# Retention attention in 64-token sub-chunks on quadrants of the PE array, four units moved to the second token chunk, and every queue's order planned and pinned

## The chip, the cores and the metric

The kernel runs on one core of a Trainium2 chip. The metric is the device time of one execution in microseconds (us). The kernel before takes 617.95 us, the median of 3 runs (617.76 to 618.27).

## What is computed

The reference is a retention layer (attention with an exponentially fading state) for 2 batches, 8 heads, 768 tokens and a head size of 64, followed by two feed-forward layers over all 1536 tokens. Weights and inputs are given in float64 and split on the chip into words that the engines can use.

```python
for t in range(S):                       # retention, per batch and head
    state = gamma * state + outer(k[t], v[t])
    y[t] = scale * q[t] @ state
x = y.transpose(...).reshape(1536, 512)
h = x @ moe_w_in                         # 512 -> 2048
g = softplus(h); x = g @ moe_w_out       # 2048 -> 512
h = x @ moe2_w_in
g = h * clip(h + 3, 0, 6) / 6; out = g @ moe2_w_out
```

## The kernel before

The token dimension is cut in three chunks of 512 (c = 0, 1, 2) for the feed-forward layers, and in 12 units of 128 tokens for the attention; units 0 to 3 make chunk 0, units 4 to 7 chunk 1, units 8 to 11 chunk 2. Units 0 to 5 belong to the first batch, 6 to 11 to the second.

**Feed-forward.** A layer m runs, for each chunk, 16 steps f of 128 hidden columns. `gemm1` makes one bank of hidden values from 12 matmuls of 128 x 512 (four k-slices, three products of high and low parts), then ScalarE (ACT) and VectorE (DVE) make g and its parts `hi` and `lo`. `gemm2` of the step two before (`LAG`) adds 12 more matmuls into four accumulating banks. A group of 12 matmuls is called a block below; there are 2 x 3 x 16 x 2 = 192 blocks, 2304 matmuls in all.

**Weights.** Each of the 64 weight tiles comes as 512 KB of float64 words (`fetch` into `raw`, three buffers) and goes through `convert`: ACT scales the upper word, DVE clamps it, shifts it, merges the sign and the upper bits of the lower word (four DVE instructions, two of them with one operand and two with two), ACT writes the high part. The low part is a subtraction on GpSimd (POOL) for the first eight tiles; for the others ACT writes the negative and a DMA queued on POOL adds `w` onto it. The 32 tiles of layer 0 are all needed in the time of chunk 0.

**Attention.** For a unit, PE transposes k and q (4 matmuls of 128 x 128 each), `scores` multiplies them per head on 64 of the array's 128 rows, `carry` multiplies q with the state `bd`, `intra` multiplies the masked scores `pt` with v on 64 of the array's columns, and `state` makes the unit's own k-v product. DVE masks the scores, scales the result by `tq_sb` and adds to the state; POOL scales v by `tk_sb` (units 2 to 11), fades the state and makes `x_lo`.

**Order.** Units 0 to 3 run before the first block, in program order (`InOrder` pins each instruction while `nc.on` is true). After that the scheduler of the tile framework chooses each engine's order by the priority of the program, with units 4 to 11 written into the first eight steps of the feed-forward. Its pools give out buffers as they come free.

The trace names one line (L31, the wrapper of `InOrder`) for nearly every instruction; the tiles' names tell them apart. An fp32 matmul of the attention stands in the trace as two records, so 8 matmuls of `scores` are 16 records.

Of the kernel before, what the change touches and what calls it, by code (L numbers as in the profile page):

```python
# [16 lines left out]
P = 128  # L17

# [3 lines left out]
class InOrder:  # L22


    class Engine:
        def __init__(self, owner, engine):
            self.owner, self.engine = owner, engine

        def __getattr__(self, op):
            def call(*args, **kwargs):  # L30
                ins = getattr(self.engine, op)(*args, **kwargs)  # L31
                return self.owner.tc.keep_in_program_order(ins) if self.owner.on else ins
            return call

    def __init__(self, tc):
        self.tc, self.on = tc, True
        for e in ("tensor", "vector", "scalar", "gpsimd", "sync"):
            setattr(self, e, self.Engine(self, getattr(tc.nc, e)))
# [3 lines left out]
def kernel(ctx, tc, q, k, v, w1_in, w1_out, w2_in, w2_out, tq, tk, tc_, tg, out):  # L42
    nc = InOrder(tc)
# [9 lines left out]
    chunks1 = [(0, 0, 512), (1, 0, 512), (2, 0, 512)]  # L53
    chunks2 = [(0, 0, 512), (1, 0, 512), (2, 0, 512)]
    LAG = 2
    EARLY = 4
# [3 lines left out]
    xpool = ctx.enter_context(tc.tile_pool(name="xpool", bufs=1))  # L60
    x_hi = [xpool.tile([P, KD, CH], F32R, name=f"x_hi{c}") for c in range(NT // CH)]
    x_lo = [xpool.tile([P, KD, CH], F32R, name=f"x_lo{c}") for c in range(NT // CH)]

    win_p = ctx.enter_context(tc.tile_pool(name="win", bufs=NF))
    wout_p = ctx.enter_context(tc.tile_pool(name="wout", bufs=NF))
    psum = ctx.enter_context(tc.tile_pool(name="psum", bufs=1, space=PSUM))
    raw_p = ctx.enter_context(tc.tile_pool(name="raw", bufs=3))
    cv_p = ctx.enter_context(tc.tile_pool(name="cv", bufs=2))

    w_in_t, w_out_t, raws = {}, {}, {}  # L70
    words = {0: (w1_in.bitcast(U32), w1_out.bitcast(U32)), 1: (w2_in.bitcast(U32), w2_out.bitcast(U32))}

    def fetch(m, o, f):
        raw = raw_p.tile([P, CH, 2], U32, tag="raw", name="raw")
        src = words[m][o]
        if o:
            nc.sync.dma_start(out=raw.rearrange("p n t -> p (n t)"), in_=src[f * P:(f + 1) * P, :])
        else:
            nc.sync.dma_start(out=raw.rearrange("p (k n) t -> p k (n t)", k=KD),
                              in_=src[:, 2 * f * P:2 * (f + 1) * P].rearrange("(k p) f -> p k f", p=P))  # L80
        raws[m, o, f] = raw

    def convert(m, o, f):

        raw = raws.pop((m, o, f))
        low, y = raw[:, :, 0], raw[:, :, 1]

        w = cv_p.tile([P, CH], U32, tag="w", name="w")
        nc.scalar.activation(y.bitcast(F32), y.bitcast(F32), AF.Copy, scale=2.0 ** -112)
        nc.vector.tensor_scalar(y.bitcast(F32), y.bitcast(F32), -TOP, TOP, ALU.max, ALU.min)  # L90
        nc.vector.tensor_scalar(w, y, 3, None, ALU.logical_shift_left)
        nc.vector.scalar_tensor_tensor(w, y, 0x80000000, w, ALU.bitwise_and, ALU.bitwise_or)
        nc.vector.scalar_tensor_tensor(w, low, 29, w, ALU.logical_shift_right, ALU.bitwise_or)
        t = (wout_p if o else win_p).tile([P, 2, CH], F32R, tag="w", name="w_parts")
        if done[1] < 2 * EARLY:
            nc.scalar.activation(t[:, 0], w.bitcast(F32), AF.Copy)
            nc.gpsimd.tensor_tensor(t[:, 1], w.bitcast(F32), t[:, 0].bitcast(F32), ALU.subtract)
        else:
            nc.scalar.activation(t[:, 1], w.bitcast(F32), AF.Copy, scale=-1.0)
            nc.gpsimd.dma_start(out=t[:, 1].bitcast(F32), in_=w.bitcast(F32), accum_op=ALU.add)  # L100
            nc.scalar.activation(t[:, 0], w.bitcast(F32), AF.Copy)
        if o:
            w_out_t[m, f] = t
        else:
            w_in_t[m, f] = t.rearrange("p a (k n) -> p a k n", k=KD)

    NU = B * NCH
# [4 lines left out]
    done = [0, 0]  # L112

    def fetch_weights(n):
        while done[0] < min(len(order), n):
            fetch(*order[done[0]])
            done[0] += 1

    def feed(n):

        n = min(n, len(order))
        while done[1] < n:
            fetch_weights(done[1] + (1 if nc.on else 2))
            convert(*order[done[1]])
            done[1] += 1

    banks = psum.tile([P, 8, CH], F32, name="banks")
    free = list(range(8))

    def bank(hold=False):  # L130

        i = free.pop(0)
        if not hold:
            free.append(i)
            return banks[:, i, :]
        return i, banks[:, i, :]

    def release(i):
        free.append(i)

    def first(f):
        return EARLY + 2 * (f + 1) - max(0, f + 1 + EARLY - NF)

# [11 lines left out]
    while s < n_steps:  # L155
        step(s)
        s += 1


def attention(ctx, tc, nc, q, k, v, tq, tk, tcc, tg, x_hi, x_lo, CH, bank, feed, fetch_weights):  # L160
# [86 lines left out]
    def state(u):  # L247
        b, i = units[u]
        if i == NCH - 1:
            return  # L250
# [211 lines left out]
```

## Time and profile before

| | |
|---|---|
| time, median of 3 runs | 617.95 us |
| span of the profiled execution | 613.8 us |
| PE (matmul) busy | 598.1 us |
| DVE busy | 351.8 us |
| ACT busy | 275.9 us |
| POOL busy | 103.4 us |
| first feed-forward matmul | 34.24 us |
| last attention matmul ends | about 120 us |
| last matmul ends | about 610.1 us |

The page lists no time of the profiled execution beside its span; the span runs from the first to the last instruction, and the median of the runs is 4.15 us above it. Busy shares are averages over very different stages: up to 34 us there is attention alone, up to about 125 us attention mixed with the first feed-forward steps and the weights' conversion, then feed-forward alone. A PE that is shown busy can still be slowed by its clock or by matmuls that use half of the array.

### The profile page before, as it was taken

Reading aid. Unit: us, or ns where it says so; the run is one execution under the profiler, and the core shown is the slowest. Engines: PE = TensorE matmul, PEld = TensorE weight load, DVE = VectorE, ACT = ScalarE, POOL = GpSimd, SP = SyncE. Lnnn points to the kernel's source line nnn. Section 1 sums busy time; section 2 is a strip of 40 time slices with the busy share of each in tenths; the row PEclk is TensorE's granted clock in tenths of the full one; section 3 lists DMA queues with packets and bytes.
Section 4 is the critical chain, followed back from the end, with each engine's and each line's share of the span. In section 5 each row is a group of like instructions: output and inputs, shape, how many; then the busy total and the mean of one; then the engine's idle time right before and its main releaser. Section 6 shows DMA issues by size and latency. Waiting matters only on the chain.

```text
span 613.8 us, 7743 instructions
## 1 busy us (share of the span) xinstructions
PE 598.1 (97%) x2963; PEld 491.2 (80%) x2963; DVE 351.8 (57%) x583; ACT 275.9 (45%) x473; POOL 103.4 (17%) x110
## 2 busy tenths in 40 slices
PE   7988999999999999999999999999999999999997
PEld 6865778788788888888887878888888888888886
DVE  4589999999773334376667798832322222322223
ACT  3355475678563333465556687722222222222220
POOL 1745664432100000011111122200000000000000
PEclk9998999999999999999999999999999999999999
DMA  9998888799600000045566689600100000100001
GB/s 193 236 229 211 219 197 208 192 217 227 159 32 0 1 0 1 9 111 119 140 180 154 162 208 262 125 7 1 68 1 0 1 1 0 70 1 1 0 1 69
DMA packets 69510, 61.60 MB, mean 100 GB/s; under 512 B 40032, under 2 KB 56672, under 8 KB 69472
## 3 DMA queue, kind: packets, MB, share of 16 engines
q1 hardware_dynamic: 61408, 46.42, 26.6%
q0 software_dynamic: 8064, 14.68, 14.6%
q8 instruction: 23, 0.38, 0.3%
q14 instruction: 15, 0.12, 0.1%
HBM read 43.26 MB, written 3.15 MB: 76 GB/s over the span
## 4 chain that ended last, share of the span: by engine, by line
PE 66%; DVE 13%; issue 7%; DMA 6%; ACT 3%; POOL 2%; SPq 1%; DVEq 0%; POOLq 0%; ACTq 0%
PE banks L31 66%; DVE w L31 6%; DMA raw<-in_moe_w_in_dram 3%; DVE raw L31 2%; POOL w_parts L31 2%; DMA w_parts<-w 2%; DVE g L31 1%; SPq L31 1%; DVE pt L31 1%; DMA q<-in_q_dram 1%; DVE lo L31 1%; ACT e L31 1%; DVE e L31 1%; ACT raw L31 1%; ACT w_parts L31 1%
## 5 line engine op out<-in xcount | busy, mean ns | idle before, releaser
L31 PE MATMUL banks<-x_hi,w_parts 128*128 128x512 f32 x768 | 253.9, 391 | 2.4 <-POOL w_parts L31 1.2
L31 PEld LDWEIGHTS banks<-x_hi,w_parts 128*128 128x128 f32 x768 | 143.8, 188 | 34.4 <-POOL w_parts L31 2.1
L31 PE MATMUL banks<-x_lo,w_parts 128*128 128x512 f32 x384 | 149.6, 390 | 0.0
L31 PE MATMUL banks<-hi,w_parts 128*128 128x512 f32 x384 | 129.4, 397 | 0.9 <-POOL w_parts L31 0.8
L31 PE MATMUL banks<-w_parts,hi 128*128 128x512 f32 (+1 forms) x386 | 118.4, 388 | 0.7 <-DVE g L31 0.7
L31 DVE SCALAR_TENSOR_TENSOR g<-e,banks 128x512 f32<-128x512 f32 x48 | 33.0, 687 | 123.3 <-ACT e L31 123.3
L31 DVE SCALAR_TENSOR_TENSOR w<-raw,w 128x512 uint32<-128x512 uint32 x128 | 94.3, 738 | 1.6
L31 DVE TENSOR_TENSOR lo<-g,hi 128x512 fp32r<-128x512 f32 x96 | 66.3, 690 | 48.9 <-ACT hi L31 48.6
L31 POOL DMA_DIRECT2D w_parts<-w x56 | 49.3, 880 | 251.9 <-DVE e L31 98.7
L31 ACT ACTIVATE hi<-g 128x512 fp32r<-128x512 f32 x96 | 60.5, 630 | 65.0 <-DVE g L31 61.6
L31 ACT ACTIVATE e<-banks,three 128x512 f32<-128x512 f32 x48 | 32.9, 686 | 125.7 <-PE banks L31 125.7
L31 ACT ACTIVATE w_parts<-w 128x512 fp32r<-128x512 f32 x120 | 70.4, 625 | 39.2 <-DVE w L31 39.0
L31 PEld LDWEIGHTS banks<-hi,w_parts 128*128 128x128 f32 x384 | 72.8, 190 | 17.6 <-POOL w_parts L31 1.5
L31 PEld LDWEIGHTS banks<-w_parts,hi 128*128 128x128 f32 x386 | 72.3, 188 | 16.0 <-DVE g L31 1.1
L31 PEld LDWEIGHTS banks<-x_lo,w_parts 128*128 128x128 f32 x384 | 72.1, 188 | 14.9
L31 PE MATMUL banks<-lo,w_parts 128*128 128x512 f32 x192 | 75.6, 394 | 0.4 <-DVE lo L31 0.4
L31 PE MATMUL banks<-w_parts,lo 128*128 128x512 f32 (+1 forms) x193 | 74.9, 388 | 0.0
L31 DVE SCALAR_TENSOR_TENSOR e<-g,banks 128x512 f32<-128x512 f32 x48 | 32.7, 682 | 27.5 <-ACT g L31 27.5
L31 DVE TENSOR_TENSOR g<-g,e 128x512 f32<-128x512 f32 x48 | 34.4, 717 | 23.9 <-ACT e L31 23.5
L31 ACT ACTIVATE raw<-raw 128x512 f32<-128x512 f32 x64 | 42.2, 669 | 12.7 <-DMA raw<-in_moe_w_in_dram 12.7
L31 ACT ACTIVATE g<-banks 128x512 f32<-128x512 f32 x48 | 28.2, 587 | 36.5 <-PE banks L31 36.5
L31 PEld LDWEIGHTS banks<-lo,w_parts 128*128 128x128 f32 x192 | 36.5, 190 | 8.9 <-DVE lo L31 1.5
(45 smaller groups left out, 401.1 us busy)
## 6 DMA issues: line engine op xcount, KB each, us to landing
raw<-in_moe_w_in_dram SPq DMA_DIRECT2D x32, 512.0 KB, 4.2
raw<-in_moe_w_out_dram SPq DMA_DIRECT2D x32, 512.0 KB, 4.6
w_parts<-w POOLq DMA_DIRECT2D x56, 256.0 KB, 4.9
q<-in_q_dram SPq DMA_DIRECT2D x12, 256.0 KB, 5.3
v<-in_v_dram SPq DMA_DIRECT2D x12, 256.0 KB, 4.9
k<-in_k_dram SPq DMA_DIRECT2D x11, 256.0 KB, 5.3
out_dram<-ob SPq DMA_DIRECT2D x11, 256.0 KB, 2.0
k<-in_k_dram SPq DMA_DIRECT2D x2, 128.0 KB, 2.8
```

Of the source, the lines that this page charges most:

```text
L31: ins = getattr(self.engine, op)(*args, **kwargs)
```

## The change

The same outputs are computed by another arrangement:

- A class `Plan` takes the place of `InOrder`. Every piece of work is a task with an engine, a cost, the tasks it comes after, a due time, and the buffers it takes and gives. `Plan.run` walks through the tasks engine by engine, chooses the next by due time among those that could start, and emits it; every instruction's order is pinned. Buffers are fixed tiles (`room`), numbered by the plan.
- Attention: each unit of 128 tokens is worked in two halves of 64 tokens. `scores`, `product` (before: `state`), `carry` and `inner` (before: `intra`) are each 16 matmuls of 64 x 64 x 64, placed on quadrants of the array: two row halves times two column halves. In `scores`, `product` and `inner` four consecutive matmuls use four quadrants; in `carry` they use the two quadrants on the diagonal, for one half of the tokens and then the other. The state lives in compact [128, 4, 64] tiles and is updated twice per unit (`middle`, `total`, `faded`).
- Units 4 to 7 are spread over chunk 0 of layer 0, four gaps between blocks per unit; units 8 to 11 are spread over chunk 1.
- POOL does no arithmetic: v's scaling, the state's fading and `x_lo` are on DVE; the low part of 15 of the 32 layer-0 tiles is a DVE subtraction, and the other 17 and all of layer 1 go by the accumulating DMA. POOL still issues those DMAs.
- Weights: for three tiles of four, ACT makes the lower word's bits (`bits`) and DVE merges with two two-operand instructions and one clamp; the fourth keeps the four DVE instructions of before. The first three weights' loads stand ahead of the loads of v and k for unit 3. Layer-1 weights are fetched one or two per step from chunk 2 of layer 0 on.
- Softplus takes one DVE instruction with one operand and one with two ahead of `lo`, where it took two with two.

```diff
-class InOrder:
...
+class Plan:
...
-    def decayed(u):
-        vs = wk.tile([P, H, D], F32, tag="vs" + "0" * (u < START), name="vs", bufs=2)
-        (nc.vector if u < 2 else nc.gpsimd).tensor_tensor(
-            vs, nat["v", u], tk_sb.rearrange("p (h o) -> p h o", o=1).to_broadcast([P, H, D]), ALU.mult)
...
-        for j in range(NP):
-            for g in range(2):
-                r = slice(D * g, D * (g + 1))
-                nc.tensor.matmul(sc[g][:, j, :], kT[r, j, :], qT[r, j, :])
...
-        nc.gpsimd.tensor_tensor(lo, on, hi.bitcast(F32), ALU.subtract)
...
+    def BY_DVE(n):
+        return n < 6 or n < 2 * NF and n % 3 == 1
+
+    def BITS(n):
+        return n % 4 != 1
...
+    spread(range(START, FIRST), 0, 1.0)
+    spread(range(FIRST, NU), 2 * NF, 1.0)
...
+        t1 = nc.add("ACT", 0.57, scale, [t0], use - tail - 3.5)
+        t3 = nc.add("DVE", TS, clamp, [t1], use - tail - 2.5)
+        if BITS(number):
+            t2 = nc.add("ACT", 0.65, bits, [t0], use - tail - 3.0, take=cv)
+            t4 = nc.add("DVE", TT, sign, [t3, t2], use - tail - 2.0)
+            t5 = nc.add("DVE", TT, shift, [t4], use - tail - 1.3, give=[raw_k])
...
+        def scores():
+            for p in range(NP):
+                for j in range(2):
+                    for g in range(2):
+                        nc.tensor.matmul(sub(sc, g)[part[j], p, :], tile_of("kT")[part[g], p, part[j]], tile_of("qT")[part[g], p, part[j]])
...
+        def product():
+            for h in range(H):
+                g, p = h % 2, h // 2
+                for j in subs:
+                    nc.tensor.matmul(sub(ds, j)[part[g], p, :], tile_of("k")[part[j], h, :], tile_of("vs")[part[j], h, :])
...
+        def carry():
+            for j in range(int(first), 2):
+                w = at_slot(mid[1] if j else ("end", u - 1))
+                for p in range(NP):
+                    for g in range(2):
+                        nc.tensor.matmul(bank(("oc", u))[part[g], p, part[j]], w[part[g], p, :], tile_of("qT")[part[g], p, part[j]])
...
+        def inner():
+            for h in range(H):
+                g, p = h % 2, h // 2
+                for j in range(2):
+                    nc.tensor.matmul(sub(oi, j)[part[g], p, :], tile_of("vs")[part[j], h, :], tile_of("pt").rearrange(
+                        "p n (g t) -> p g n t", g=2)[part[j], g, p, :])
```

The order that the plan makes is shown at three places. The first is PE's queue in the attention of the first four units, before any feed-forward matmul. Before, one unit stands like this: `qT,kT` is scores, `ident,k` and `ident,q` are transposes, `qT,bd` is carry, `pt,vs` is intra and `vs,k` is state.

```order
L31 MATMUL banks<-qT,kT 128x128 x8
L31 MATMUL banks<-ident,k 128x128 x4
L31 MATMUL banks<-ident,q 128x128 x4
L31 MATMUL banks<-qT,bd_112 128x128 x4
L31 MATMUL banks<-pt,vs 64x128 x8
L31 MATMUL banks<-vs,k 128x128 x4
```

Now the same place, for unit 2 (its scores are the first row) and the start of unit 3; `st` is the state.

```order
L41 MATMUL banks<-qT_0_130,kT_0_129 64x64 x16
L41 MATMUL banks<-vs_0_132,k_2_125 64x64 x16
L41 MATMUL banks<-ident,q_0_120 128x128 x4
L41 MATMUL banks<-qT_0_130,st_136 64x64 x8
L41 MATMUL banks<-qT_0_130,st_137 64x64 x8
L41 MATMUL banks<-pt_0_134,vs_0_132 64x64 x16
L41 MATMUL banks<-ident,k_0_123 128x128 x4
L41 MATMUL banks<-vs_1_133,k_0_123 64x64 x16
L41 MATMUL banks<-qT_1_131,kT_0_129 64x64 x16
```

A unit's 24 matmuls of half or full array width became 64 of a quarter, the k-v product moved ahead of the carry, and unit 3's transpose of k stands behind all of unit 2.

The second place is PE's queue in the middle of chunk 0, where unit 5's scores stand. Before:

```order
L31 MATMUL banks<-qT,kT 128x128 x4
L31 MATMUL banks<-hi,w_parts 128x512
L31 MATMUL banks<-lo,w_parts 128x512
L31 MATMUL banks<-qT,kT 128x128 x4
L31 MATMUL banks<-qT,bd_113 128x128 x4
L31 MATMUL banks<-pt,vs 64x128
L31 MATMUL banks<-vs,k 128x128 x4
L31 MATMUL banks<-pt,vs 64x128 x7
```

Now, between the last matmul of one block and the first of the next but one:

```order
L41 MATMUL banks<-x_hi_66,w_84 128x512
L41 MATMUL banks<-qT_1_131,kT_0_129 64x64 x16
L41 MATMUL banks<-qT_1_131,st_138 64x64 x8
L41 MATMUL banks<-qT_1_131,st_136 64x64 x8
L41 MATMUL banks<-pt_1_135,vs_1_133 64x64 x16
L41 MATMUL banks<-hi_109,w_87 128x512
```

The scheduler had split the scores into two runs, each on one row half, with feed-forward matmuls between them; now each part of a unit stands whole, between blocks.

The third place is DVE's queue in chunk 0, where weights are converted beside the softplus. Before (`raw` and `w` are a weight's words, `e` and `g` the softplus):

```order
L31 SCALAR_TENSOR_TENSOR e<-g,banks 128x512
L31 TENSOR_SCALAR w<-raw 128x512
L31 TENSOR_SCALAR raw<-raw 128x512
L31 SCALAR_TENSOR_TENSOR w<-raw,w 128x512
L31 TENSOR_TENSOR g<-g,e 128x512
L31 TENSOR_SCALAR w<-raw 128x512
L31 SCALAR_TENSOR_TENSOR w<-raw,w 128x512 x2
L31 TENSOR_TENSOR lo<-g,hi 128x512
```

Now (`cv` is the word being merged, `w` the finished tile whose low part DVE subtracts):

```order
L41 TENSOR_SCALAR raw_0_72<-raw_0_72 128x512
L41 SCALAR_TENSOR_TENSOR cv_1_76<-raw_0_72,cv_1_76 128x512 x2
L41 TENSOR_TENSOR w_93<-cv_0_75,w_93 128x512
L41 TENSOR_SCALAR e_104<-g_106 128x512
L41 TENSOR_TENSOR vs_1_133<-v_1_127,small 128x512
L41 TENSOR_SCALAR raw_1_73<-raw_1_73 128x512
L41 TENSOR_SCALAR cv_3_78<-raw_1_73 128x512
L41 SCALAR_TENSOR_TENSOR g_106<-g_106,e_104 128x512
```

The shift of most weights left DVE, while the subtraction of the low part and the scaling of v came to it. From the first feed-forward matmul to the end of chunk 0 DVE's queue now holds 122 instructions with two operands (128 x 512) and 65 that are one-operand or 256 wide.

## Rows read from the trace of the kernel before

**Rows 1.** The page's part 1: busy time, share of the span, instructions.

```profile
PE 598.1 (97%) x2963; PEld 491.2 (80%) x2963; DVE 351.8 (57%) x583; ACT 275.9 (45%) x473; POOL 103.4 (17%) x110
```

**Rows 2.** Windows view by stage: window, length, engines' busy us, granted PE clock, DMA share.

```profile
0.00:34.20 34.20, 29.99 (x292) 26.06 (x293) 19.84 (x35) 10.96 (x18) 15.21 (x25) 1.00 0.94 201
34.20:56.20 22.00, 18.01 (x124) 13.71 (x122) 20.27 (x29) 12.93 (x25) 11.50 (x9) 1.00 1.07 269
56.20:63.00 6.80, 6.74 (x25) 4.53 (x26) 6.80 (x11) 2.49 (x5) 4.55 (x4) 0.50 0.54 159
63.00:125.00 62.00, 59.55 (x396) 47.92 (x395) 59.24 (x101) 39.96 (x73) 33.51 (x32) 1.00 0.83 199
125.00:164.50 39.50, 39.35 (x174) 32.24 (x172) 35.42 (x66) 29.39 (x54) 10.78 (x12) 1.00 0.90 211
164.50:358.10 193.60, 192.57 (x845) 158.21 (x845) 113.30 (x190) 98.29 (x172) 16.48 (x19) 1.00 0.34 81
358.10:610.10 252.00, 251.94 (x1113) 208.54 (x1113) 96.19 (x155) 81.84 (x133) 11.35 (x13) 1.00 0.17 43
```

**Rows 3.** The chain that ended last: start, us, what; its two long PE stretches.

```profile
164.54 114.33 PE banks L31 x503
...
358.13 251.96 PE banks L31 x1113
```

**Rows 4.** Timeline of PE: unit 3's scores to unit 4's, and the first feed-forward matmul.

```profile
22.74 1.16 PE L31 MATMUL banks<-qT,kT 64*128 64x128 f32 x16
23.84 0.66 PE L31 MATMUL banks<-ident,k 128*128 128x128 f32 x4
24.33 0.60 PE L31 MATMUL banks<-ident,q 128*128 128x128 f32 x4
24.77 1.06 PE L31 MATMUL banks<-qT,bd 128*128 128x128 f32 x8
25.75 1.09 PE L31 MATMUL banks<-pt,vs 128*64 128x128 f32 x16
26.78 1.16 PE L31 MATMUL banks<-vs,k 128*128 128x128 f32 x8
27.86 1.16 PE L31 MATMUL banks<-qT,kT 64*128 64x128 f32 x16
...
34.24 0.47 PE L31 MATMUL banks<-x_hi,w_parts 128*128 128x512 f32 x1
```

**Rows 5.** Timeline of PE from 27.85 to 27.89 us: the first two records of scores.

```profile
27.86 0.38 PE L31 MATMUL banks<-qT,kT 64*128 64x128 f32 x2
```

**Rows 6.** Timeline of PE: scores in two runs between feed-forward matmuls.

```profile
68.16 0.39 PE L31 MATMUL banks<-hi,w_parts 128*128 128x512 f32 x1
68.48 1.16 PE L31 MATMUL banks<-qT,kT 64*128 64x128 f32 x8
69.57 0.50 PE L31 MATMUL banks<-hi,w_parts 128*128 128x512 f32 x1
69.91 0.39 PE L31 MATMUL banks<-lo,w_parts 128*128 128x512 f32 x1
70.23 1.16 PE L31 MATMUL banks<-qT,kT 64*128 64x128 f32 x8
```

**Rows 7.** Timeline of DVE while POOL computes nothing: start, duration, instruction.

```profile
132.84 0.69 DVE L31 TENSOR_TENSOR lo<-g,hi 128x512 fp32r<-128x512 f32 x1
133.44 0.68 DVE L31 SCALAR_TENSOR_TENSOR w<-raw,w 128x512 uint32<-128x512 uint32 x1
134.05 0.42 DVE L31 TENSOR_SCALAR w<-raw 128x512 uint32<-128x512 uint32 x1
134.38 0.42 DVE L31 TENSOR_SCALAR raw<-raw 128x512 f32<-128x512 f32 x1
```

**Rows 8.** Groups of DVE by form, 63 to 125 us, then 125 to 164.5 us.

```profile
L31 DVE SCALAR_TENSOR_TENSOR w<-raw,w 128x512 uint32<-128x512 uint32 x31 | 25.6, 831 | 0.3
...
L31 DVE SCALAR_TENSOR_TENSOR w<-raw,w 128x512 uint32<-128x512 uint32 x23 | 15.8, 687 | 0.3
```

**Rows 9.** Groups of DVE by form, 28.9 to 164.5 us: the clamp, one per weight.

```profile
L31 DVE TENSOR_SCALAR raw<-raw 128x512 f32<-128x512 f32 x34 | 18.8, 561 | 1.4 <-ACT raw L31 1.4
```

More of the change, by code (lines that the diff above doesn't have):

```diff
@@ L17, with __init__ @@
 P = 128
+HALF = P // 2
 TOP = float(np.uint32((255 << 20) - 1).view(np.float32))
-class InOrder:
+class Plan:
+    LAG = {"PE": 0.30, "DVE": 0.12, "ACT": 0.16, "POOL": 0.16, "SP": 0.0}
+    NEAR = {"PE": 0.5, "DVE": 0.15, "ACT": 0.15, "POOL": 0.3, "SP": 0.0}
+    class Task:
+        def __init__(self, n, eng, cost, fn, after, due, take, give, load):
+            self.n, self.eng, self.cost, self.fn, self.after = n, eng, cost, fn, [a for a in after if a is not None]
+            self.due, self.take, self.give, self.load = due, list(take), list(give), load
+            self.done = None
@@ new lines, with room, at_slot @@
+    x_hi = [fixed.tile([P, KD, CH], F32R, name=f"x_hi{c}") for c in range(NC)]
+    x_lo = [fixed.tile([P, KD, CH], F32R, name=f"x_lo{c}") for c in range(NC)]
+    slots, kinds = {}, {}
+    def room(name, n, shape, dtype, within=None, later=()):
+        nc.pool(name, n, later)
+        slots[name] = {i: (within or fixed).tile(shape, dtype, name=f"{name}_{i}") for i in range(n)}
+        kinds[name] = shape, dtype
+    def at_slot(key):
+        name, i = nc.slot[key]
+        if name == "bank":
+            return banks[:, i, :]
+        if i not in slots[name]:
+            slots[name][i] = late_p.tile(*kinds[name], name=f"{name}_{i}")
+        return slots[name][i]
@@ L130, in bank @@
[L130 to L142, printed above, removed]
-    step, last, n_steps = moe(ctx, tc, nc, out, x_hi, x_lo, w_in_t, w_out_t, chunks1, chunks2, NF, KD, DM, CH, LAG, feed, first, bank, release)
-    s = 0
-    with ExitStack() as actx:
-        unit = attention(actx, tc, nc, q, k, v, tq, tk, tc_, tg, x_hi, x_lo, CH, bank, feed, fetch_weights)
-        for u in range(CH // P, NU):
-            begin, end = unit(u)
-            begin()
-            step(s, True, False)
-            end()
-            step(s, False, True)
-            s += 1
@@ new lines, with table, both, sub @@
+    begin = -100.0
+    arena = [("arena", j) for j in range(LATE)]
+    def table(dst, src, when):
+        return nc.add("SP", 0.45, lambda: nc.sync.dma_start(out=dst, in_=src), [], when, load=1.3 if dst is tq_sb else 0.1)
+    def both(keys):
+        a, b = sorted(nc.slot[x][1] for x in keys)
+        return banks[:, a:b + 1:b - a, :NP * HALF].rearrange("p x (n t) -> p x n t", n=NP)
+    def sub(keys, j):
+        i = sorted(nc.slot[x][1] for x in keys)[j]
+        return banks[:, i, :NP * HALF].rearrange("p (n t) -> p n t", n=NP)
@@ L426, in _tables @@
+    halves = [slice(0, CH // 2), slice(CH // 2, CH)]
+    for s in range(len(G)):
+        gemm1(s)
+        if s >= LAG:
+            gemm2(s - LAG, [s - LAG])
+    gemm2(len(G) - LAG, [len(G) - LAG + i for i in range(LAG)])
+    nc.run(LOG)
+    holds[0].close()
+LOG = None
 def _tables(H, S, D):
```

680 lines of the change are left out of this document (390 added, 290 removed).

## The prediction

> **What bounds the kernel now.** I read the page's busy times first, then the windows by stage, then the chain of waits, then the timelines of PE and DVE. PE is busy 97% of the span [rows 1], so the question is what this time is made of. The chain's two long PE stretches hold 503 + 1113 matmuls in 114.33 + 251.96 us [rows 3], 0.2267 us each; the 2304 feed-forward matmuls therefore need 522.2 us and the change touches none of them. Four units of attention come ahead of the first of them, at 34.24 us, and one unit takes PE 5.12 us (scores at 22.74, the next unit's at 27.86) [rows 4]. The other eight cost 8 x 5.12 = 41.0 us, less about 0.6 us that stands ahead of 34.24, so 40.4. After the last matmul 3.7 us are left (613.8 - 610.1). The account is 34.2 + 522.2 + 40.4 + 3.7 = 600.5 us, and the span of 613.8 has 13.3 us more. The windows say where they are [rows 2]: PE idles 4.0 us between 34.2 and 56.2, 2.5 us between 63 and 125, 1.0 us between 164.5 and 358.1; from 56.2 to 63.0 the granted clock is 0.50 (1.2 GHz), half of 6.8 us lost; and three units have their scores in two runs, eight records in 1.09 us where sixteen could go [rows 6], about 1.1 us each. That makes 7.5 + 3.4 + 3.3 = 14.2, near enough. So everything that can be won lies ahead of 125 us: the start, the attention on PE, and the stage where DVE is busy 59.2 of 62 us beside it [rows 2].
>
> **Attention on PE.** The first two records of scores, on the two row halves, stand together in 0.38 us [rows 5], and sixteen records take 1.10 us to the next block's start [rows 4]: eight rounds of two, 0.1375 us a round with the entry. The new matmuls have half the columns. If four of them run on four quadrants as two halves do now, a round costs half, 0.069 us, and 16 matmuls (32 records, eight rounds of four) cost 0.55 us for scores, for the product and for `inner`; `carry` uses two quadrants, sixteen rounds, 1.10 us. The transposes stay at 0.93 us (23.84 to 24.77) [rows 4]. Sum 0.93 + 3 x 0.55 + 1.10 = 3.68 us for a unit, against 5.12. No row shows four quadrants; the bounds for a block are 0.55 us and, if only two ever run together, 1.10 us, which is today's price. I take the lower, because the rows show halves of both kinds, of rows in scores and of columns in `intra` (sixteen records in 1.03 us), at twice the full array's pace (eight records of carry in 0.98). Between feed-forward blocks each of the four parts also pays the return: 0.34 instead of 0.23 us after a run of scores (69.57 to 69.91) [rows 6], 0.4 us per unit. So 4.1 us per unit there, 8 x 4.1 = 32.8 us, less the transposes and product that are ordered ahead of the first block (1.9) and half a product of the last unit (0.3): 30.6 us.
>
> The Trainium skill ("TensorE: Matmul & The Clock Gate", section on 56 ns) says that matmuls never start closer than about 25 ns. By that the 32 records of a block would take 0.8 us and the eight units some 6 us more than I count; the pair inside 0.38 us [rows 5], whose records last 0.27 to 0.37 us, speaks against such a floor between different parts of the array.
>
> **The start.** The first block needs unit 3's result. Ahead of its v and k the queue of SP now has twelve tiles of 256 KB and the table, 3.4 MB, and three weights, 1.6 MB. At the 201 GB/s of the first 34 us, with the DMA engines 94% busy [rows 2], 5.0 MB land at about 25 us. From there a transpose 0.46, ACT's copy 0.6, scores 0.55, mask 0.68, `inner` 0.55, sum 0.68, high part 0.63, low part 0.69 make 4.9 us, with some 0.1 us at each of seven hand-overs 5.6. DVE has three weights to convert in this time on the same pinned queue, 12.9 us of work between 18.5 and 32 us, which I take to add 1.5 us. First block at 32 us, against 34.2; bounds 30 and 35. The work that hid the loads of weights, PE's dense attention, is thinner, so the start goes from PE-bound to DMA-bound, and PE has a hole of some 5 us between unit 2 and unit 3. The clock fell here once before, after a stretch in which PE was idle 4.0 of 22 us [rows 2]; I expect it to fall in the hole, which costs the first blocks 2.5 us (before: 3.4 us for 6.8 us at half).
>
> **Chunk 0: DVE.** DVE's new work looks like more (v's scaling, `x_lo`, the fading, 15 low parts), and it is not. Undisturbed, a two-operand instruction takes 0.60 us from start to start and a one-operand one 0.34 [rows 7]. From the first block to the end of chunk 0 its queue holds 122 of the former and 65 of the latter or half-wide: 73.2 + 22.1 = 95.3 us. PE's work in the same stretch is 32 blocks of 12 x 0.2267 = 2.72 us, 87.0, plus four units, 4 x 4.1 - 1.9 = 14.5: 101.5 us. DVE is covered, at 94%. It would not be at today's durations: the two-operand instruction lasts 831 ns in the stage where POOL computes and 687 ns after it [rows 8]; with no arithmetic on POOL I take the lower. This is what "no GpSimd arithmetic" buys: 31 + 34-odd instructions at some 0.1 to 0.14 us. What is queued behind a DVE instruction that waits (for ACT's copy, a bank, a weight) is now everything, since the order is pinned; the ones waiting for that are PE's next block and the release of the three `raw` buffers. Today this stage has 6.5 us of PE idling [rows 2]. I take half of it, 3.5 us; bounds 0 and, at today's pace of weights, the first rival below.
>
> **The rest.** Units 8 to 11 stand in chunk 1, where today DVE is 59% busy (113.3 of 193.6) [rows 2]; their DVE work of about 4 us each fits, and their loads start when the last layer-0 weights have left `raw`, so they are not late by more than the one block that stands between. ACT gets `bits` for 24 tiles and loses one reader of the scores: it stays below PE. The 1.0 us of idling at the change of layers I leave as it is. Layer 1, the tail and the feed-forward matmuls are the same.
>
> **Sum.** 32.0 + 522.2 + 30.6 + 3.7 = 588.5 us, plus 2.5 (clock), 3.5 (chunk 0) and 1.0 (change of layers) = 595.5 us of span. The median of the runs stands 4.15 us above the profiled span (617.95 against 613.8), so 599.7; I say 599.5.
>
> **Rivals.** *Everything hides:* the plan's order leaves no waits in chunk 0 and the clock does not fall: 588.5 + 1.0 + 4.15 = 593.7, down to 591 with a start at 30 us. For it: DVE needs 95.3 of 101.5 us; against it: such a tight stage never ran without waits here.
>
> *The weights keep their pace:* today 34 clamps fall in 135.6 us [rows 9], 3.99 us per weight. With three `raw` buffers, a landing, two ACT and three DVE visits in a pinned order the pace may stay. Then 29 weights after the first three, from 24 us, take 115.7 us to 139.7, the last blocks of chunk 0 end at about 143, and 160 blocks (435.2), four units (16.1), the change of layers and the tail follow: 599 of span, 603; with another 10% of waiting, 613. For it: three buffers as before; against it: POOL's disturbance and one DVE instruction per weight are gone.
>
> *`carry` does not pair:* its two diagonal quadrants write one bank, and no row has two row halves in one bank (today's scores put them in two). Then `carry` costs 2.2 us, 1.1 more per unit, 8 x 1.1 = 8.8: 608. The Trainium skill ("TensorEngine Tiling (Array Packing)", on PSUM pressure) says that row tiles cannot access the same bank at once; the trace of before neither shows nor denies it.
>
> *Slower: the quadrants go one at a time.* If each of the 32 records of a block needs the 0.069 us alone, a block is 2.2 us, a unit 0.93 + 8.8 + 0.4 = 10.1, 6.0 more than I count: 8 x 6.0 = 48 us, and the start becomes PE-bound at four times 9.7, some 7 us later: about 654. The change breaks even when a unit costs 18.5 / 8 = 2.3 us more than my 4.1, that is a block at 1.13 us and not 0.55 to 1.10 (twice that for `carry`). Against it: rows 5.
>
> That the change does not do what it says, four at a time, is the middle of this: all blocks at 1.10 us and `carry` at 1.10 give 1.65 us more per unit, 13 us, 612.7.
>
> **Chances.** The forecast, 595 to 604: 0.47. Everything hides, 589 to 595: 0.18. Weights' pace, 603 to 613: 0.14. `carry` unpaired, about 608: 0.07. Two at a time, about 613: 0.05. One at a time, about 654, or waits of the pinned order that add 20 us or more: 0.09. The range from 590 to 613 leaves out the last and the lowest part of the second, about 0.15. A difference of 0.2% (1.2 us) is what a measurement of this kernel can tell: faster than 616.7 has 0.89, within it 0.02, slower 0.09.
>
> **What would show it.** The scores' sixteen matmuls should stand in about 0.55 us of PE's timeline and `carry` in 1.1; the first feed-forward matmul at 32 us; the granted clock at 0.50 for some us between 22 and 36; DVE's two-operand group near 690 ns in chunk 0; PE idle 3 to 4 us from the first block to about 139 us, where chunk 1 begins. The prediction is wrong if a block takes over 1.1 us, if `raw` cycles at 4 us a weight, or if PE idles in chunk 1 behind units 8 to 11.

## The result, and the profile after

The kernel after takes 609.88 us (median of 4 runs, 609.53 to 611.77) where the kernel before takes 617.86: ratio 0.9887, 95% interval 0.986 to 0.9914. That is 8.0 us faster; 18.4 were forecast. The profiled execution took 611.77 us at a span of 610.0, the longest of the four: its clock fell twice, at 23.3 and at 88.1 us, for a mean of 0.992, where the other three have 0.997.

The page's part 1 of after, against [rows 1]: PE lost 14 us of busy time, POOL only issues DMAs, ACT gained 28 us.

```profile
PE 584.2 (96%) x3891; PEld 477.8 (78%) x3891; DVE 334.7 (55%) x584; ACT 303.9 (50%) x516; POOL 44.5 (7%) x57
```

The windows by stage of after, in the columns of [rows 2]: the start, chunk 0 in two parts, and the part of chunk 1 that has attention.

```profile
0.00:34.40 34.40, 23.84 (x588) 21.12 (x588) 24.13 (x49) 14.19 (x24) 1.08 (x8) 0.90 0.98 224
34.40:63.00 28.60, 25.76 (x254) 19.55 (x246) 27.33 (x51) 22.41 (x39) 2.98 (x3) 1.00 0.85 224
63.00:149.20 86.20, 80.48 (x615) 64.02 (x611) 73.16 (x138) 68.17 (x122) 12.32 (x14) 0.98 0.71 177
149.20:213.60 64.40, 61.74 (x722) 48.61 (x720) 30.88 (x56) 22.13 (x38) 0.00 (x0) 1.00 0.22 55
```

PE idles 10.6 us in the start, 2.8 and 5.7 us in chunk 0, and 2.7 us in chunk 1, where neither DVE nor ACT is busy for half of the time. That last number is the odd one.

The quadrants work as forecast. PE's timeline of after, unit 7 between two feed-forward blocks (start, length, instruction): scores take 0.51 us, carry 1.00, inner 0.87 with the return, where [rows 4] has 1.10, 0.98 and 1.03.

```profile
98.00 0.69 PE L41 MATMUL banks<-qT,kT 64*64 64x64 f32 x32
98.51 1.11 PE L41 MATMUL banks<-qT,st 64*64 64x64 f32 x32
99.51 0.94 PE L41 MATMUL banks<-pt,vs 64*64 64x64 f32 x32
100.38 0.50 PE L41 MATMUL banks<-hi,w 128*128 128x512 f32 x1
```

PE's timeline of after from the hole of the start to the first feed-forward block, which stood at 34.24 in [rows 4] (the bracket is the idle time ahead, and its releaser):

```profile
24.64 1.11 PE L41 MATMUL banks<-ident,k 128*128 128x128 f32 x4 [4.94 <-DMA k<-in_k_dram]
25.68 1.13 PE L41 MATMUL banks<-vs,k 64*64 64x64 f32 x32
26.59 1.08 PE L41 MATMUL banks<-qT,kT 64*64 64x64 f32 x32
27.45 1.93 PE L41 MATMUL banks<-qT,st 64*64 64x64 f32 x32
30.23 0.69 PE L41 MATMUL banks<-pt,vs 64*64 64x64 f32 x32 [0.85 <-DVE pt L41]
...
33.83 0.69 PE L41 MATMUL banks<-vs,k 64*64 64x64 f32 x32 [1.45 <-DVE vs L41]
34.46 0.50 PE L41 MATMUL banks<-x_hi,w 128*128 128x512 f32 x1
```

Unit 3's k lands at 24.6 as forecast (25), but its chain to the first block takes 9.8 us. The granted clock was 0.50 from 23.3 to 30.1 us, so unit 3's carry lasts 1.93 us, where unit 7's above lasts 1.11; the wait for `pt` is DVE's mask, and the next paragraph is about that.

**The odd wait.** Timeline of after in chunk 1, unit 8, DVE and PE (its buffers are named `cv` and `raw` there, since units 8 to 11 use the space of the weights): scores start at 156.68 and the next block follows at 157.31, DVE has nothing else to do from 158.55 on, and its mask starts at 160.37, having waited 1.81 us for PE.

```profile
156.68 0.69 PE L41 MATMUL banks<-cv,raw 64*64 64x64 f32 x32
157.27 1.28 DVE L41 TENSOR_TENSOR x_lo<-banks,x_hi 128x512 fp32r<-128x512 f32 x2
...
159.94 0.39 PE L41 MATMUL banks<-x_hi,w 128*128 128x512 f32 x1
160.37 0.69 DVE L41 TENSOR_TENSOR cv<-banks,small 128x512 f32<-128x512 f32 x1 [1.81 <-PE banks L41]
161.11 1.08 PE L41 MATMUL banks<-cv,st 64*64 64x64 f32 x29 [0.78 <-DVE cv L41]
```

What ended at 160.3 was the feed-forward block behind scores. The mask reads its two score banks with one instruction, through `both`: a slice with a stride, from bank a to bank b. For unit 8 the plan hands out banks 2 and 5, and the block in question writes bank 3. In the trace no record of these scores updates the semaphore that the mask waits for; its last update ahead of the mask comes at 160.34, with this block's last matmul. Of the twelve masks, six read banks that are not neighbours (units 3, 6 and 8 to 11), and the last update ahead of each of the six is that of matmuls it doesn't need: carry's for unit 3, a feed-forward block's for the others. Ahead of the six on neighbouring banks it is that of scores. The sums `on` of units 7 and 9 to 11 read `inner`'s banks the same way and have the same wait, 1.2 to 2.9 us. The theory is that these false waits (waits for matmuls whose banks the instruction does not read) took most of what is missing; the rivals are the start (hole and clock) and the load of DVE or ACT in chunk 0.

### The profile page after: what moved, and what is told of

Same layout as the page of the kernel before. It is cut to its first block, busy times and chain, and to the rows that moved or that the text cites. A ratio compares the mean times of both kernels' runs of the same rounds, so it can differ in the third digit from the quotient of the medians.

```text
span 610.0 us, 9620 instructions
## 1 busy us (share of the span) xinstructions
PE 584.2 (96%) x3891; PEld 477.8 (78%) x3891; DVE 334.7 (55%) x584; ACT 303.9 (50%) x516; POOL 44.5 (7%) x57
## 4 chain that ended last, share of the span: by engine, by line
PE 82%; DVE 7%; DMA 6%; issue 2%; ACT 2%; SPq 1%; DVEq 0%; ACTq 0%
PE banks L41 82%; DVE cv L41 3%; DMA raw<-in_moe_w_in_dram 2%; DMA k<-in_k_dram 2%; DMA raw<-in_moe_w_out_dram 1%; DVE g L41 1%; DVE raw L41 1%; SPq L41 1%; ACT raw L41 1%; ACT cv L41 0%; DVE lo L41 0%; ACT g L41 0%; DVE e L41 0%; DVE w L41 0%; DMA out_dram<-e 0%
## 5 line engine op out<-in xcount | busy, mean ns | idle before, releaser
L41 PE MATMUL banks<-x_hi,w 128*128 128x512 f32 x768 | 254.7, 393 | 4.9 <-ACT kT L41 2.3
L41 PEld LDWEIGHTS banks<-x_hi,w 128*128 128x128 f32 x768 | 144.8, 189 | 36.9 <-ACT kT L41 2.5
L41 PE MATMUL banks<-x_lo,w 128*128 128x512 f32 x384 | 150.3, 391 | 0.0
L41 PE MATMUL banks<-hi,w 128*128 128x512 f32 x384 | 127.9, 395 | 0.8 <-DVE w L41 0.3
L41 PE MATMUL banks<-w,hi 128*128 128x512 f32 (+1 forms) x386 | 118.3, 388 | 0.0
L41 DVE SCALAR_TENSOR_TENSOR cv<-raw,cv 128x512 uint32<-128x512 uint32 x128 | 87.5, 690 | 7.1 <-ACT cv L41 4.6
L41 PEld LDWEIGHTS banks<-hi,w 128*128 128x128 f32 x384 | 72.0, 188 | 17.6 <-ACT hi L41 0.8
L41 PEld LDWEIGHTS banks<-w,hi 128*128 128x128 f32 x386 | 72.4, 188 | 14.9
L41 PEld LDWEIGHTS banks<-x_lo,w 128*128 128x128 f32 x384 | 72.4, 189 | 14.5
L41 PE MATMUL banks<-lo,w 128*128 128x512 f32 x192 | 75.2, 391 | 1.2 <-DVE lo L41 1.2
L41 PE MATMUL banks<-w,lo 128*128 128x512 f32 (+1 forms) x193 | 74.9, 388 | 0.0
```

The source lines that it names most:

```text
L41: return self.plan.tc.keep_in_program_order(getattr(self.engine, op)(*args, **kwargs))
```

## Experiments

The kernel before stood at 615.2 to 616.1 us on the chips of these runs. Ratios are to it. A visit below is PE's stay at attention between two feed-forward matmuls, from the start of the one to the start of the other, less the 0.23 us of a matmul. Units 4 to 7 have theirs in chunk 0, units 8 to 11 in chunk 1.

**The kernel after again**, for a base on the same chips.

> The kernel after once more, unedited, on the chip of the runs beside it. Theory: ratio to the kernel before 0.989 as the first time, 608.3 us where before takes 615.2. If it lies nearer to 0.98, the gain of the run with the split reads has to be taken smaller.

Measured 610.24 us, 0.9898 (0.9862 to 0.9935). The two measurements agree; 0.989 is the base below, 610 us.

**Split reads: one instruction for each bank where banks are apart.**

```diff
+    def apart(keys):
+        a, b = sorted(nc.slot[x][1] for x in keys)
+        return b > a + 1
...
+            if apart(sc):
+                for x in range(2):
+                    nc.vector.tensor_tensor(to[:, x], sub(sc, x), m[:, 0].to_broadcast([P, NP, HALF]), ALU.mult)
+            else:
+                nc.vector.tensor_tensor(to, both(sc), m.to_broadcast([P, 2, NP, HALF]), ALU.mult)
```

> Where a unit's pair of banks is not adjacent (unit 3's and 6's masks, units 8 to 11, seven pairs for the mask and five for the sum), the one strided DVE instruction that reads both is made two, one for each bank; order and buffers stay. Theory (the strided read is held until matmuls are done that write a bank lying between the two): DVE's mask in chunk 1 starts right after scores and no longer after the next block, the three long carry-and-inner visits there fall from 2.49 to about 1.75 us, unit 3's mask starts 1.5 us sooner and the first block with it, unit 6 gains 0.4: 4 us less, 606 us, ratio to the kernel after 0.993. Rival (DVE is late there by its own queue): the visits stay at 2.49 us, and the time at 610 within 1 us.

Measured 601.02 us, 0.9756 (0.9727 to 0.9786): 9 us less than after, more than twice what was expected. (The pairs that are apart are six for the mask and four for the sum, not the seven and five of the expectation.) The same place as above, in the timeline of this kernel: the mask comes right behind scores, and carry waits for nothing. The scores now have updates of their own, at 151.51 and 151.55, one for each bank.

```profile
150.78 0.69 PE L41 MATMUL banks<-cv,raw 64*64 64x64 f32 x32
151.37 1.28 DVE L41 TENSOR_TENSOR x_lo<-banks,x_hi 128x512 fp32r<-128x512 f32 x2
152.57 0.75 DVE L41 TENSOR_TENSOR cv<-banks,small 128x256 f32<-128x256 f32 x2
154.36 1.08 PE L41 MATMUL banks<-cv,st 64*64 64x64 f32 x29
```

DVE's groups in chunk 1, the mask in after and with split reads (count, busy, mean ns, and idle time ahead): eight short instructions cost 0.2 us more than four long ones, and 10.6 us of DVE's waiting are gone.

```profile
L41 DVE TENSOR_TENSOR cv<-banks,small 128x512 f32<-128x512 f32 x4 | 2.8, 692 | 12.3 <-PE banks L41 12.3
```

```profile
L41 DVE TENSOR_TENSOR cv<-banks,small 128x256 f32<-128x256 f32 x8 | 3.0, 418 | 1.7 <-PE banks L41 1.7
```

Most of the rest of the gain is one place in chunk 0. In after, unit 6's mask (banks 2 and 5) holds DVE for 3.31 us; ACT's next instruction waits for that mask, a weight's conversion slips on both engines, `kT` of unit 7 is copied late behind it, and PE, which needs the bank that `kT` is copied from, stands for 2.27 us. DVE, ACT and PE in turn:

```profile
79.17 0.69 DVE L41 TENSOR_TENSOR pt<-banks,small 128x512 f32<-128x512 f32 x1 [3.31 <-PE banks L41]
```

```profile
79.95 0.60 ACT L41 ACTIVATE g<-banks 128x512 f32<-128x512 f32 x1 [3.38 <-DVE pt L41]
...
85.96 0.68 ACT L41 ACTIVATE raw<-raw 128x512 f32<-128x512 f32 x1 [0.28 <-DMA raw<-in_moe_w_in_dram]
86.54 0.58 ACT L41 ACTIVATE kT<-banks 128x512 f32<-128x512 f32 x1
```

```profile
87.17 0.50 PE L41 MATMUL banks<-x_hi,w 128*128 128x512 f32 x1 [2.27 <-ACT kT L41]
```

With split reads the same copy is at 83.09, and PE's wait is 0.29 us:

```profile
83.73 0.50 PE L41 MATMUL banks<-x_hi,w 128*128 128x512 f32 x1 [0.29 <-ACT kT L41]
```

**Split reads in units 8 to 11 alone.**

```diff
-        return b > a + 1
+        return b > a + 1 and keys[0][2] >= FIRST
```

> The split reads in units 8 to 11 alone; units 3 and 6 keep the strided read. Theory (each strided read is held by a block that writes a bank between, and each place costs for itself): chunk 1's three visits of 2.49 us fall to 1.64 and two transpose visits of 1.17 to 0.80, 4 us less than the kernel after: 606 us where after takes 610; the waits around unit 6 (2.02 us in its carry visit, 3.3 in the transposes at 83 us) stay. Rival (the gain of the split reads came from chunk 0 or from the start): 609 or more.

Measured 606.88 us, 0.9837 (0.9794 to 0.988): 3.4 us less than after. The long visits of chunk 1 (carry with inner, and transposes) fell from 2.49 and 1.17 to 1.64 and 0.80 us, those around unit 6 stayed at 2.03 and 3.26. Of the 9 us, then, some 3.5 lie in chunk 1 and 5.5 around units 3, 6 and 7, where a held DVE also holds the weights.

**The clock of the start: forty transposes in the hole.**

```diff
             def go():
+                for x in range(40 if n == "k" and u == START - 1 else 0):
+                    nc.tensor.transpose(bank((n + "P", u))[:, x % NP, :], ident, ident)
                 for p in range(NP):
```

> Forty transposes of the identity stand ahead of unit 3's transpose of k, in the same bank, so that PE is busy in its 4.9 us hole; nothing else is changed and order and buffers stay. Theory (the hole brings the half clock, and the half clock stretches unit 3's chain): the granted clock stays 1.00 from 23.3 to 30.1 us, unit 3's scores, product and carry take 0.55, 0.55 and 1.0 us instead of 0.9, 0.9 and 1.9, the first block comes at 32.3 instead of 34.46: 2 us less, 608 us. Rival (chunk 0 is set by DVE and ACT, so that an earlier first block only waits more): first block earlier, time at 610 within 1 us. Third: the clock falls all the same, and nothing moves.

Measured 608.75 us, 0.9894 (0.9859 to 0.9929): no change that the intervals show. PE's timeline: the clock stayed at 1.00 until 87.7 us and carry took 1.11, but the forty run past the landing of k (unit 3's k is turned 1.2 us later than in after), and DVE's waits are what they were.

```profile
21.43 4.59 PE L41 MATMUL banks<-ident 128*128 128x128 f32 x40
25.86 0.60 PE L41 MATMUL banks<-ident,k 128*128 128x128 f32 x4
...
29.69 0.69 PE L41 MATMUL banks<-pt,vs 64*64 64x64 f32 x32 [0.86 <-DVE pt L41]
...
33.29 0.69 PE L41 MATMUL banks<-vs,k 64*64 64x64 f32 x32 [1.45 <-DVE vs L41]
33.91 0.50 PE L41 MATMUL banks<-x_hi,w 128*128 128x512 f32 x1
```

From unit 3's transpose to the first block 8.05 us pass, against 9.82 in after: the half clock cost this chain 1.8 us, of which the later transpose takes 1.2 back. PE's last wait ahead of the block is the same in both, 1.45 us for `vs` on DVE's pinned queue. Twenty transposes on top of split reads:

> On the kernel with the split reads, twenty transposes of the identity ahead of unit 3's transpose of k. Theory (with the strided read gone, unit 3's chain is set by PE at half clock): the clock stays 1.00 through the start, unit 3's carry and inner take 1.6 us and not 2.8, the first block comes at 32.5 instead of 33.67: 600 us. Rival (unit 3's chain is set by DVE's pinned queue, with the conversion of weights in it): the first block comes at 33.3 or later, the time within 0.6 us of 601.

Measured 600.44 us, 0.9727 (0.9689 to 0.9765). The clock stayed at 1.00, and the first block came at 32.87 (33.67 with split reads alone), between the two expectations:

```profile
24.98 0.66 PE L41 MATMUL banks<-ident,k 128*128 128x128 f32 x4 [1.38 <-DMA k<-in_k_dram]
...
32.87 0.50 PE L41 MATMUL banks<-x_hi,w 128*128 128x512 f32 x1
```

Here k landed 0.8 us later than in the profiled execution of split reads alone (24.19), and the chain behind it took 7.9 us, against 9.5 there. The interval of the time overlaps that of split reads alone, so the gain, if any, is within 2 us. Of the kernels that leave no work out it has the lowest median.

**All loads of k, q, v ahead of the first weight** (`AHEAD = 0` in place of 3).

> All loads of k, q, v of units 0 to 3 stand ahead of the first weight. Theory (the landing of unit 3's k and v sets the start): k of unit 3 lands at about 18 us, the hole of 4.9 us is gone, the first block comes at 28 us instead of 34.5, and chunk 0 gets no worse: 604 us. Rival (the conversion of 32 weights on DVE and ACT sets the end of chunk 0, and it starts later now): the first block comes earlier but waits grow in chunk 0; the 32nd block ends at 149 us or later, the time is 610 or more, up to 613.

Measured 615.42 us, 0.9976 (0.9948 to 1.0004): nearly all of the change's gain is gone. The rival was right in kind, and its 613 still too low. Neither it nor the theory saw that the first block would come later: the hole is gone, PE goes on with units 4 and 5, and the first block stands at 36.8 us, behind ACT's writing of the first `w` at 36.13; weights come late after that too, and chunk 1 begins at 153.9. PE's waits, summed by releaser (us, times, longest):

```profile
PE banks L41 <- DMA w<-cv: 5.8, 2, 3.4
PE banks L41 <- ACT kT L41: 2.5, 1, 2.5
```

**Less work for DVE and for ACT in chunk 0.** The first run leaves out `sign` on the kernel after, the second `bits` on the kernel with split reads, the third `sign` there, the fourth both there.

```diff
-            t4 = nc.add("DVE", TT, sign, [t3, t2], use - tail - 2.0)
+            t4 = nc.add("DVE", TT, sign if m else (lambda: None), [t3, t2], use - tail - 2.0)
...
-            t2 = nc.add("ACT", 0.65, bits, [t0], use - tail - 3.0, take=cv)
+            t2 = nc.add("ACT", 0.65, bits if m else (lambda: None), [t0], use - tail - 3.0, take=cv)
```

> DVE's first merging instruction (sign) is left out for the 24 layer-0 tiles that have it: the weights lose their sign, and 24 x 0.69 = 16.6 us of DVE's work before 140 us are gone; order and buffers stay. Theory (DVE's load sets the 11.7 us of waits in chunk 0): they fall by half or more, 603 us or less. Rival (ACT's pinned order, banks and late loads set them): 1.5 us less at most, 608.5 or more.

Measured 607.14 us, 0.9862 (0.9832 to 0.9892): 2 to 3 us less than after, between the two expectations.

> On the kernel with the split reads, ACT's instruction for the lower word's bits is left out for the 24 layer-0 tiles that have it, so that weights lose their lowest bits: 24 x 0.75 = 18 us of ACT's work before 140 us are gone; DVE's merge keeps its cost, order and buffers stay. Theory (ACT's pinned order sets the waits that are left in chunk 0: 2.7 us for ACT's read of the hidden bank, 1.4 in the transpose visit at 66 us): 3 us less, 598 us. Rival (loads and DVE set them): 1 us less at most.

Measured 600.45 us, 0.9733 (0.9691 to 0.9775), about 1 us less than split reads and not clear of the noise, with 18 us of ACT's work gone: the rival.

> On the kernel with the split reads, DVE's sign is left out for the 24 layer-0 tiles that have it (the weights lose their sign): 16.6 us of DVE's work before 140 us are gone, order and buffers stay. Theory (the chain of waits runs over DVE from 37 to 68 us and over the weights' loads from 80 to 138 us, so DVE's queue sets the first half of what is left): 3 us less than split reads, 598 us. Rival (what is left is the plan's order of banks and hand-overs): within 1 us of 601.

Measured 598.26 us, 0.9702 (0.9676 to 0.9728): 3 us less than split reads, as the theory has it.

> On the kernel with the split reads, both DVE's sign and ACT's bits are left out for these 24 tiles (the weights lose sign and lowest bits): 16.6 us of DVE's and 18 us of ACT's work. Theory (the two engines' queues together set the 8 us of waits that are left in chunk 0, each covering for the other when one alone is relieved): 5 us less than split reads or more, 596 us or under. Rival (loads through three raw buffers, banks and order set them): at most 2.5 us less, 598.5 or more.

Measured 598.59 us, 0.9709 (0.968 to 0.9738): no less than with DVE alone relieved, so the two queues don't cover for each other. Leaving out DVE's `sign` is worth 3 us of what is left, leaving out ACT's `bits` nothing beside it. It takes load off DVE and also makes each weight's conversion shorter by one instruction (the last clamp of layer 0 comes at 128.8 us instead of 133.8); these runs don't tell the two apart. The waits of PE in chunk 0 that stay when DVE is relieved are for a read of a bank (`g` is read from a hidden bank by ACT, and for `on` from inner's banks by DVE), in the view of waits from 34.5 to 143 us:

```profile
PE banks L41 <- ACT g L41: 2.1, 2, 1.1
PE banks L41 <- DVE g L41: 1.2, 1, 1.2
PE banks L41 <- ACT kT L41: 0.3, 1, 0.3
```

**Another order for units 4 to 7**, on split reads: spread over all of chunk 0, then packed closer with fewer low parts on DVE.

```diff
-    spread(range(START, FIRST), 0, 1.0)
+    spread(range(START, FIRST), 1, 1.75)
```

> On the kernel with the split reads, units 4 to 7 are spread over all of chunk 0 (one part of a unit behind every 1.75 blocks, from the second block on) instead of its first half; the plan makes new orders from that. Theory (DVE and ACT are full from 40 to 70 us, because attention, conversion and feed-forward meet there, and have slack behind 95 us): the waits of chunk 0 fall from 8 us to 4 or less, and unit 4's product no longer stands ahead of the first block (1 us): 596 us. Rival (the weights' conversion sets chunk 0's length whatever the order): within 1.5 us of 601.

Measured 607.13 us, 0.9844 (0.9805 to 0.9884): 5 to 6 us more, against both expectations. PE's waits moved to the feed-forward chain and to unit 3 (1.9 us for ACT's `hi`, 1.7 for DVE's `lo`, 1.6 for `vs`).

> On the kernel with the split reads, units 4 to 7 are packed closer (one part behind every 0.7 blocks instead of every block) and the low part of layer-0 tiles is DVE's for the first four and one in four, not the first six and one in three (12 tiles instead of 15). Theory (DVE and ACT set what is left of chunk 0's waits, and the plan's own times, which put this 1.6 us earlier, hold): 599.5 us. Rival (an order as good as any other): within 1 us of 601, either side.

Measured 603.18 us, 0.9764 (0.9723 to 0.9806): the ratio is that of split reads (0.9756), as the rival says.

**GpSimd gets its arithmetic back**, on split reads.

```diff
-        vs = task("DVE", TT, lambda: nc.vector.tensor_tensor(
+        ve, vn = ("DVE", nc.vector) if u < 2 else ("POOL", nc.gpsimd)
+        vs = task(ve, TT if u < 2 else 1.2, lambda: vn.tensor_tensor(
...
-        o3 = task("DVE", TT, lambda: nc.vector.tensor_tensor(lo, of("on"), hi.bitcast(F32), ALU.subtract), [o2], need - 0.8,
+        o3 = task("POOL", 1.2, lambda: nc.gpsimd.tensor_tensor(lo, of("on"), hi.bitcast(F32), ALU.subtract), [o2], need - 0.8,
```

> On the kernel with the split reads, GpSimd gets its arithmetic back: v's scaling from unit 2 on, the state's fading and the low part of x, some 33 instructions; the plan makes its order with that. Theory (GpSimd slows DVE beside it, and its own instructions take 1.2 to 1.4 us instead of 0.7): DVE's two-operand instruction goes from 0.69 to about 0.73 us in chunk 0 and the first block comes later by 1 us; 2 to 4 us more: 604. Rival (DVE is relieved of 20 us of work and chunk 0's waits shrink): 1 to 3 us less: 599.

Measured 606.22 us, 0.9814 (0.9776 to 0.9852): 4 to 5 us more than split reads alone, as the theory has it. The plan made another order for this kernel, and the clock fell twice in its profiled execution (for 10.2 and 3.4 us), so how much of the loss is DVE's slowing is not shown. DVE's two-operand group from 35 to 125 us, in after and with GpSimd at work; [rows 8] had 831 and 687 ns.

```profile
L41 DVE SCALAR_TENSOR_TENSOR cv<-raw,cv 128x512 uint32<-128x512 uint32 x47 | 32.0, 689 | 1.4 <-ACT cv L41 0.2
```

```profile
L41 DVE SCALAR_TENSOR_TENSOR cv<-raw,cv 128x512 uint32<-128x512 uint32 x50 | 37.1, 746 | 2.3 <-ACT cv L41 0.4
```

**One quadrant after the other**, on split reads: the four loops go through all heads of one quadrant before the next.

```diff
-            for p in range(NP):
-                for j in range(2):
-                    for g in range(2):
+            for j in range(2):
+                for g in range(2):
+                    for p in range(NP):
                         nc.tensor.matmul(sub(sc, g)[part[j], p, :], tile_of("kT")[part[g], p, part[j]], tile_of("qT")[part[g], p, part[j]])
```

> On the kernel with the split reads (601.0 us), the matmuls of scores, product, inner and carry go out one quadrant after the other instead of quadrants in turn; the work and the order of blocks stay. Theory (only neighbours in PE's queue on different quadrants run together): each block takes 32 x 0.069 = 2.2 us instead of 0.55 (carry instead of 1.0), a unit 6.0 us more, eight units 48 us and some 7 us in the start: about 655 us. Rival (PE looks further ahead, or a record costs its 16 ns on any quadrant): within 2 us of 601. Between them, at 1.1 us a block: 615.

Measured 623.02 us, 1.0103 (1.0033 to 1.0173): 22 us more than split reads alone, and slower than the kernel before. Scores of unit 8, alone between two blocks, now take 1.47 us to the next block's start, against 0.63 in after (156.68 to 157.31):

```profile
157.40 1.54 PE L41 MATMUL banks<-cv,raw 64*64 64x64 f32 x32
158.87 0.50 PE L41 MATMUL banks<-hi,w 128*128 128x512 f32 x1
```

A unit of chunk 1 costs 2.75 us more in its visits (0.84 for scores, 0.84 for the product, 1.07 for carry and inner together). Between the profiled executions the first block comes 4.5 us later (38.21), chunk 0 is 5.7 us longer and the part behind it 10.7, some 21 us in all. The theory had the sign, and was more than twice too high in the size: it let each record stand alone. In the trace the first four records of these scores start 58 ns apart, as it has it, but behind them a round of 58 ns holds one record or two, 32 records in 23 rounds, so the run of one quadrant overlaps that of the next in part. The order in which the quadrants are written is thus worth more here than the whole change won.

## Why the prediction was right in kind and wrong in size

The forecast's own account, beside what the profiled executions of after and of split reads give for each term (us; "other" is the time that is not feed-forward matmuls):

| term | forecast | after | split reads |
|---|---|---|---|
| first block | 32.0 | 34.5 | 33.7 |
| other time in chunk 0 (attention, waits, clock) | 20.5 | 27.9 | 22.8 |
| other time from chunk 1 on | 17.1 | 21.4 | 17.6 |
| 2304 matmuls at 0.2267 | 522.2 | 522.3 | 522.3 |
| tail | 3.7 | 3.9 | 3.8 |
| span | 595.5 | 610.0 | 600.2 |

(Chunk 0 of after: unit 8's transposes start at 149.41, the first block at 34.46, less 384 x 0.2267 = 87.05; the last matmul ends at 606.10.)

**Right.** The price of a unit on quadrants: with the false waits gone, the four units of chunk 1 take 15.5 us in their visits, against 16.1 forecast. The landing of unit 3's k, the hole of 4.9 us and the fall of the clock. DVE's two-operand instruction at 689 ns without arithmetic on GpSimd. The matmuls. `carry` pairs (1.00 us), so that rival is out, and so are two or one at a time.

**A rival that was nearer than I gave it.** Two signs that the prediction named for its being wrong both came: PE idles in chunk 1 behind units 8 to 11, and `raw` cycles at 4 us a weight. *The weights keep their pace* had 3.99 us for each weight and the last conversion at 139.7 us, at a chance of 0.14. DVE's timeline of after, the clamp of the third weight and of the last of layer 0, is just that, 3.94 us for each of the 29 between ([rows 9] for the clamp before):

```profile
25.41 0.42 DVE L41 TENSOR_SCALAR raw<-raw 128x512 f32<-128x512 f32 x1
...
139.64 0.42 DVE L41 TENSOR_SCALAR raw<-raw 128x512 f32<-128x512 f32 x1
```

Its reason was only in part the one it named: with split reads, on the same buffers and the same order, the last clamp is at 133.77, 3.70 us a weight, so a held DVE holds the conversion. What sets the 3.70 that are left is not shown.

The Trainium skill ("TensorE: Matmul & The Clock Gate", "Wait — 56ns, not 53.3ns?") says that matmuls never start closer than about 25 ns. The trace disagrees for quadrants in turn: 32 records in 0.51 us (98.00 to 98.51 above) are 16 ns each, and within a round of four they start 6 or 7 ns apart.

**Wrong: the waits in chunk 0 (3.5 us) and the 1.0 us from chunk 1 on.** I took half of the old idling for the one, and for the other wrote that the units' DVE work fits beside PE, which it does. Both looked at load. What came was a new kind of wait: a read that stands for two banks and is held for those between. By the table it took 5.1 us in chunk 0 (1.7 of them the second fall of the clock, from 88.1 to 91.6 us behind the 2.27 us wait), 3.8 from chunk 1 on and 0.8 in the start, 9.7 of the 14.5 us by which the span missed; between the medians split reads are worth 9.2. The prediction did ask what is queued behind a DVE instruction that waits, and found the right victims (PE's next block, the weights); it did not ask for what each DVE instruction waits. The line `banks[:, a:b + 1:b - a, ...]` was in the code, and the banks that the plan hands out were to be had.

**Wrong, smaller: the start.** 4.9 us of chain, 0.7 of hand-overs and 1.5 for DVE were forecast, 9.8 came. The half clock that I charged to the first blocks fell on unit 3's chain instead (it ended at 30.1), and cost it 1.6 to 1.8 us: the chain takes 9.8 us in after and 8.0 with the clock held, 9.5 and 7.9 with split reads. The first block gained only 0.55 and 0.8 of that, since in both runs with the clock held unit 3's k was turned later. The 8 us that stay are still above the 7.1 forecast, with DVE's queue ahead of `vs` as PE's last wait (1.45).

**Wrong: the offset.** The 4.15 us between the median and the span of before is not a property of the chip: in after a run's time stands 1.8 us above its span (611.77 against 610.0). The profiled execution of before was simply one of its faster ones. This error went the other way and made the miss look 2.3 us smaller.

**Wrong, without effect: the break-even.** If `carry` costs twice a block, a unit has five shares, and 2.75 + 2.3 us make 1.01 us a block, not 1.13. The run with one quadrant after the other, at 2.75 us more a unit, lies beyond it and is slower than before.

**Open.** Of the 8 us of waits that split reads leave in chunk 0 (22.8 us less 14.5 of attention), leaving out `sign` takes 3, by DVE's load or by the shorter conversion. The rest stands at waits for a bank, four of which are left beside the accumulators; no run here had more, so that the banks cause it is argued only.

## What to carry to other kernels

Where the order is pinned and buffers are handed out by a program, list for each instruction what it is made to wait for, and compare it with what it reads: an access that spans two buffers with a stride can be held by everything between them, and splitting it cost 0.06 us (0.66 instead of 0.60 from start to start) where the six waits held DVE for 1.7 to 3.8 us each. An engine that idles in a stage where it has slack, and is released by PE, is the sign to look for. And an account in terms that a trace can fill in again afterwards shows in one table which term was wrong.

## What the runs showed of the hardware

Matmuls of 64 x 64 x 64 on four quadrants in turn take 16 ns a record, on two quadrants in turn 31 ns (carry, 32 records in 1.00 us), and one quadrant after the other 42 ns (0.84 us more for the 32 of scores). In all three the records start in rounds some 58 ns apart: of four, of two, and of one or two where the run of one quadrant overlaps the next one's. The first four records of a quadrant that stands alone (scores with one quadrant after the other) thus take 58 ns each, nearly four times the 16; I had reckoned with 69 ns.

The Trainium skill ("TensorEngine Tiling (Array Packing)", "Gotcha 1: PSUM Pressure") says that different row tiles cannot access the same bank at once. `carry` puts its two diagonal quadrants into one bank at 31 ns a record; the two records of a round start 7 ns apart and last over 200 ns each, so here both are under way at once. No run here has the same pair in two banks, so whether it pays for that is not shown.

The granted clock fell to 0.50 at 23.3 us, in the hole that lasts from 19.7 to 24.6, and stayed at 1.00 through the start when PE had transposes to do there.
